# First of five convolution taps taken from VectorE to ScalarE in the first six quads of a softcap attention with a gated convolution behind it

## The chip, the cores and the metric

The kernel runs on one core of a Trainium2 chip. The metric is device time in microseconds (us) of one launch. The core has five engines, each with a queue of its own that it works off in order: TensorE (PE in the profile, with its weight loads as PEld), VectorE (DVE), ScalarE (ACT), GpSimd (POOL) and SyncE (SP), which here issues nearly all DMA transfers. Engines wait for each other only through semaphores; an instruction that waits holds up all that stands behind it on its engine.

## The reference, cut to what matters

```python
# q, k, v: (8, 12, 448, 64), cap = 30
scores = cap * np.tanh(np.matmul(q, k.transpose(0, 1, 3, 2)) / np.sqrt(64) / cap)
scores = scores - np.max(scores, axis=-1, keepdims=True)
attn = np.exp(scores)
attn = attn / (np.sum(attn, axis=-1, keepdims=True) + 1e-09)
x = np.matmul(attn, v)                    # then heads side by side: (8, 448, 768)
# gated convolution, conv_w: (5, 768), w_val and w_out: (768, 768)
xp = np.concatenate([np.zeros((B, K - 1, D)), x], axis=1)
gate_pre = 0
for k in range(K):                        # K = 5 taps
    gate_pre += conv_w[k][None, None, :] * xp[:, k:k + S, :]
gate = 1.0 / (1.0 + np.exp(-gate_pre))
val = x @ w_val
out = gate * val @ w_out
```

## The kernel before

**Tiling.** Heads are worked in pairs (48 pairs, `p`), two pairs make a quad (24 quads, `s`), and three quads make one batch element (8 batches, `b`). For a pair, q and k are loaded (`qkn`) and turned by a 32x32 block transpose on DVE (`qkt`, L515). From pair 9 on, q and k are split into a high and a low part (`qkh` by ACT at L525, `qkl` by DVE at L425, a helper's line that also makes `xl` and `g_l`). TensorE makes score tiles of 128 rows into PSUM (`pss`, L542; the remaining rows of a quad at L553), ACT takes tanh (L558, and L569 for the remaining rows) and exp (L562, L573) into `pt`, DVE adds some of them up (`pa`, L586, L589), and TensorE forms the sums of the rows (`psz`, L610) and the products with v (`psa`, `psz`, L636). DVE turns the sums (`zt`, L641), inverts them (`rc`) and spreads them (L652). L660 and L663 multiply the attention output by them into `u`, the x of one quad, with channels on partitions: 2 channel chunks of 128 by 4 + 448 columns, the first 4 being the zeros ahead of the convolution. All quads but quad 1 use the same `u`.

**The convolution and the rest.** A quad's gate (`gate`, 128 x 2 x 448) is built chunk by chunk: the step `conv(s, n)` with n from 0 to 9 is tap `i = n % 5` of chunk `t = n // 5`. Tap 0 writes `gate = u * cw` (L688), taps 1 to 4 add `u * cw` (L690, a shifted window of `u`). All ten are on DVE. Beside it ACT and DVE split `u` into `xh` (L675) and `xl`. For a batch, TensorE multiplies xh and xl with `wv` into `pss` (L706 to L708), ACT takes the sigmoid of the gate (L694), DVE multiplies the two (L718), ACT and DVE split the product into `g_h` (L721) and `g_l`, and TensorE multiplies with `wo` (L741 to L743). ACT copies the result (L750), and SP stores it. PSUM has three `pss` buffers, which scores, remainder, value and output tiles use in turn.

**The weights** arrive in 12 pieces as 64-bit floats in the first 120 us and are split on the way: SP loads `w_raw`, ACT makes two pieces of it (L311, L312), and DVE the parts that TensorE reads (L315, L316, then L319, L320, L323 with `w_late`). There is one buffer of each kind, so the next load of `w_raw` starts when L316 of the piece before has read it.

**The order.** Every step stands in a table (`PAIR`, `QUAD`, `BATCH`, `ONCE`) with a number. All steps are sorted by that number and emitted in this order, and each engine keeps it as its queue. Nothing is moved afterwards. The numbers are measured in pairs: step `conv` number n of quad s comes at `2 s` plus the table's row n. For quad 2 the table's third column holds these, in the order in which they come:

```python
# n:  0         1         5         2         6         3         7 ...
#  1.321381  1.919916  2.164879  2.18007   2.209755  2.224579  2.308679
```

Quad 2 lies at 4 plus that, so its n = 5 (tap 0 of chunk 1) at 6.165 and n = 6 (tap 1 of chunk 1) at 6.210. For quad 4 (column 5) n = 5 lies at 12.279 and n = 6 at 12.400.

Of the kernel before, what the change touches and what calls it, by code (L numbers as in the profile page):

```python
# [12 lines left out]
AF = mybir.ActivationFunctionType  # L13
# [12 lines left out]
NXX, NPT, NG = 3, 8, 3  # L26
NPRE, NLATE, NPLAIN, NTWO = 3, 4, 9, 16
NADD = (0, 0, 0, 1, 2)
BY_DMA = tuple(range(4, 12))
ON_VECTOR = (0, 1, 2, 3)  # L30

# [255 lines left out]
def shifted(late, n):  # L287

    return late.bitcast(I32)[..., 1:2 * n:2]
# [91 lines left out]
def fast_path(tc, io, u0, q, k, v, w_val, conv_w, w_out, out, capt):  # L381

    nc = tc.nc
# [15 lines left out]
    with ExitStack() as ctx:  # L399
# [37 lines left out]
        cw = cpool.tile([P, KW, NCC], F32, name="cw")  # L437
# [17 lines left out]
        def late_tile():  # L455
            return wsc.tile([P, 2, 4 * NH + 2], U16, name="w_late")

        def late_load(n):
            if n in BY_DMA:
                w, g, nh, _ = wsteps[n]  # L460
                wlate[n] = late_tile()
                nc.sync.dma_start(
                    wlate[n][:, :, 1:1 + 4 * NH], quad_rows(w.bitcast(U16), g)[:, :, nh * 2 * DM:(nh + 1) * 2 * DM]
                )

        def weight_first(n):
            _, g, nh, w = wsteps[n]
            t = wsc.tile([P, 2, NH], I32, name="w_t")
            mid = None if n in BY_DMA else late_tile().bitcast(I32)[:, :, :NH]
            c = slice(2 * g, 2 * g + 2)  # L470
# [13 lines left out]
        def weight_third(n):  # L484
            last = wstate.pop(n)[2]
            if n in BY_DMA:
                last(shifted(wlate.pop(n), NH))
# [87 lines left out]
        def adds(s):  # L575
            return NADD[s] if s < len(NADD) else NT

# [76 lines left out]
        def u_of(s):  # L654
            return u1 if s == 1 else u0
# [11 lines left out]
        def late(s):  # L667
            return s >= NLATE and s % (NXX + 1) == NLATE % (NXX + 1)
# [12 lines left out]
        def conv(s, n):  # L681
            t, i = divmod(n, KW)
            if n == 0:
                gates[s] = scratch["late"].tile([P, 2, S], F32, name="gate", bufs=1) if late(s) else wk.tile([P, 2, S], F32, name="gate", bufs=NG)
            c = s % NQ * 2 + t
            g, u = gates[s][:, t], u_of(s)[:, t, i:i + S]
            if i == 0:
                nc.vector.tensor_scalar_mul(g, u, cw[:, 0, c:c + 1])  # L688
            else:
                nc.vector.scalar_tensor_tensor(g, u, cw[:, i, c:c + 1], g, ALU.mult, ALU.add)  # L690

# [77 lines left out]
        def put(table, steps, count, unit, col):  # L769
# [9 lines left out]
        ), NP, 1, column)  # L779
        put(QUAD, dict(  # L780
            rest=rest, rest_tanh=rest_tanh, rest_exp=rest_exp, sums=sums, av=av, turn_sums=turn_sums, recip=recip, spread=spread, mul=mul, x_hi=x_hi, x_lo=x_lo, conv=conv,
        ), NP // 2, 2, quad_column)
        put(BATCH, dict(
# [186 lines left out]
```

## Time and profile before

| | |
|---|---|
| median of 3 runs | 689.72 us (689.52 to 689.75) |
| profiled execution, its own time | 689.57 us |
| its span, first to last instruction | 687.7 us |
| granted TensorE clock, mean | 0.99 |
| DVE busy in the span | 560.0 us |
| ACT busy in the span | 502.1 us |

In rows of the timeline the first number is the start and the second the length, both in us, then engine, line, operation, what is written and read, and how many instructions the row merges; a bracket at the end is the time that the engine stood idle just before, and what ended it. An instruction's length is longer than its step to the next one where the two overlap. In the chain of waits a piece is start, length, and what the end hung on in that time.

### The profile page before, as it was taken

The page shows a single profiled execution, that of the slowest core. Times are in us where ns is not written, and L with a number is a line of the kernel's source. Part 1 is how long each engine was busy: PE and PEld are TensorE (multiplying, and loading weights), DVE is VectorE, ACT ScalarE, POOL GpSimd, SP SyncE. Part 2 cuts the span into 40 slices and gives each one's busy share as a digit, 9 for nine tenths or more (in the row PEclk, how much of TensorE's full clock was granted, in tenths as well). Part 3 has the DMA queues.
Part 4 walks back from the last instruction along what each step waited for, and adds up shares of the span by engine and source line. Part 5 has one row for each costly group of instructions (what it writes and reads, how often), then busy time and mean ns, then how long its engine had stood idle before and what let it go on. Part 6 is the DMA issues. An engine that isn't in the chain of part 4 may idle for free.

```text
span 687.7 us, 11825 instructions
## 1 busy us (share of the span) xinstructions
PE 659.3 (96%) x4698; PEld 467.7 (68%) x4698; DVE 560.0 (81%) x779; ACT 502.1 (73%) x538; POOL 0.4 (0%) x7
## 2 busy tenths in 40 slices
PE   4787999999999999999999999999999999999996
PEld 1221584587597686786686696876766878767996
DVE  3899999999978889987979877988879896897530
ACT  5579769889684898777797695886788785975110
POOL 0000000000000000000000000000000000000000
PEclk9899999999999999999999999999999999999999
DMA  7769888433343432250334430423235332111001
GB/s 117 166 164 218 226 223 229 96 67 60 80 91 71 91 68 67 61 104 15 68 78 91 100 68 18 106 57 68 44 65 113 80 78 39 51 38 60 0 25 72
DMA packets 235166, 60.66 MB, mean 88 GB/s; under 512 B 226400, under 2 KB 226400, under 8 KB 235104
## 3 DMA queue, kind: packets, MB, share of 16 engines
q1 hardware_dynamic: 233248, 59.61, 39.1%
q8 instruction: 39, 0.64, 0.4%
q10 hardware_dynamic: 1856, 0.23, 0.3%
q14 instruction: 23, 0.19, 0.1%
HBM read 48.79 MB, written 11.01 MB: 87 GB/s over the span
## 4 chain that ended last, share of the span: by engine, by line
PE 75%; DVE 5%; ACT 3%; DMA 1%; issue 1%; SPq 0%; DVEq 0%; ACTq 0%
PE pss L542 10%; PE psa L636 9%; PE pss L706 8%; PE pss L741 7%; PE pss L708 7%; PE pss L707 7%; PE pss L743 7%; PE pss L742 7%; PE psz L636 7%; PE psz L610 3%; PE pss L553 2%; DVE pa L586 1%; DVE gate L690 1%; ACT pt L558 1%; ACT pt L562 1%; DVE pa L589 1%
## 5 line engine op out<-in xcount | busy, mean ns | idle before, releaser
L558 ACT ACTIVATE pt<-pss,rc 128x896 f32<-128x896 f32 x144 | 140.0, 1004 | 68.5 <-PE pss L542 44.6
L562 ACT ACTIVATE pt<-pt,capt 128x896 f32<-128x896 f32 x144 | 145.6, 1042 | 0.6
L690 DVE SCALAR_TENSOR_TENSOR gate<-u,cw,gate 128x448 f32<-128x448 f32 x192 | 125.9, 674 | 1.7
L741 PE MATMUL pss<-wo,g_h 128*128 128x384 f32 x336 | 114.9, 342 | 0.0
L743 PE MATMUL pss<-wo,g_l 128*128 128x384 f32 x336 | 113.8, 339 | 0.0
L742 PE MATMUL pss<-wo,g_h 128*128 128x384 f32 x336 | 113.6, 338 | 0.0
L706 PE MATMUL pss<-xh,wv 128*128 128x448 f32 x288 | 105.9, 368 | 0.0
L708 PE MATMUL pss<-xl,wv 128*128 128x448 f32 x288 | 104.3, 362 | 0.0
L707 PE MATMUL pss<-xh,wv 128*128 128x448 f32 x288 | 104.3, 362 | 0.0
L741 PEld LDWEIGHTS pss<-wo,g_h 128*128 128x128 f32 x336 | 63.1, 188 | 9.0 <-ACT pt L558 6.4
L636 PE MATMUL psa<-pt,vn 128*32 128x448 f32 x576 | 69.2, 547 | 0.0
L636 PE MATMUL psz<-pt,vn 128*32 128x448 f32 x576 | 64.8, 541 | 1.4 <-DVE zt L641 1.4
L750 ACT COPY osb<-pss 128x768 f32<-128x768 f32 x28 | 22.3, 798 | 57.0 <-PE pss L743 56.0
L743 PEld LDWEIGHTS pss<-wo,g_l 128*128 128x128 f32 x336 | 63.1, 188 | 0.6 <-DVE g_l L425 0.6
L742 PEld LDWEIGHTS pss<-wo,g_h 128*128 128x128 f32 x336 | 63.1, 188 | 0.4 <-DVE wo L323 0.3
L706 PEld LDWEIGHTS pss<-xh,wv 128*128 128x128 f32 x288 | 54.0, 187 | 12.9 <-ACT pt L558 5.3
L515 DVE STREAM_TRANSPOSE qkt<-qkn 128x896 f32<-128x896 f32 x47 | 51.6, 1104 | 6.7 <-DMA qkn<-in_k_dram 3.8
L708 PEld LDWEIGHTS pss<-xl,wv 128*128 128x128 f32 x288 | 54.0, 188 | 3.8
L707 PEld LDWEIGHTS pss<-xh,wv 128*128 128x128 f32 x288 | 54.0, 188 | 3.5
L718 DVE TENSOR_TENSOR gate<-pss,gate 128x896 f32<-128x896 f32 x24 | 26.1, 1088 | 31.2 <-PE pss L708 31.2
L586 DVE TENSOR_TENSOR pa<-pt 128x896 f32<-128x896 f32 x42 | 45.3, 1078 | 7.5 <-ACT pt L562 7.5
L542 PE MATMUL pss<-qkh 64*128 64x448 f32 x234 | 48.4, 406 | 0.5 <-ACT pt L558 0.5
(86 smaller groups left out, 931.9 us busy)
## 6 DMA issues: line engine op xcount, KB each, us to landing
out_dram<-osb SPq DMA_DIRECT2D x28, 384.0 KB, 2.6
qkn<-in_q_dram SPq DMA_DIRECT2D x188, 56.0 KB, 2.3
qkn<-in_k_dram SPq DMA_DIRECT2D x188, 56.0 KB, 2.3
vn<-in_v_dram SPq DMA_DIRECT2D x96, 96.0 KB, 2.5
w_raw<-in_moe_w_val_dram SPq DMA_DIRECT2D x6, 768.0 KB, 4.7
w_raw<-in_moe_w_out_dram SPq DMA_DIRECT2D x6, 768.0 KB, 5.0
w_late<-in_moe_w_out_dram SPq DMA_DIRECT2D x6, 768.0 KB, 4.9
vh<-in_v_dram SPq DMA_DIRECT2D x48, 32.0 KB, 2.3
```

The lines of the kernel that those rows point to most:

```text
L542: nc.tensor.matmul(ps[:, j, :S], st[x][r, 1, c], st[y][r, 0], start=(n == 0), stop=(n == len(parts) - 1))
L558: nc.scalar.activation(st["p", i], st.pop(("s", i)), AF.Tanh, scale=rc8)
L562: nc.scalar.activation(t, t, AF.Exp, scale=capt)
L586: nc.vector.tensor_tensor(st["a"], st["p", 0] if i == 0 else st["a"], st["p", i + 1], op=ALU.add)
L636: nc.tensor.matmul(o, w, x, start=(q["n", t] == 1), stop=(q["n", t] == NT + 1))
L690: nc.vector.scalar_tensor_tensor(g, u, cw[:, i, c:c + 1], g, ALU.mult, ALU.add)
L706: nc.tensor.matmul(o[:, t, :S], w_h, xh, start=(c == 0), stop=False)
L707: nc.tensor.matmul(o[:, t, :S], w_l, xh, start=False, stop=False)
L708: nc.tensor.matmul(o[:, t, :S], w_h, xl, start=False, stop=(c == NCC - 1))
L741: nc.tensor.matmul(o[:, nh, :NH], g_h[:, d, s], w_h, start=(d == 0), stop=False)
L742: nc.tensor.matmul(o[:, nh, :NH], g_h[:, d, s], w_l, start=False, stop=False)
L743: nc.tensor.matmul(o[:, nh, :NH], g_l[:, d, s], w_h, start=False, stop=(d == NCC - 1))
```

## The change

The first tap (n = 0 and n = 5) of quads 0 to 5 becomes an ACTIVATE of kind Copy with a scale for each partition on ScalarE. It is emitted at the place where the multiply on VectorE was. The other 18 quads keep theirs. All later lines shift by 1 up to L687 and by 4 behind the new code, so L690 of before is L694 in the changed kernel, and the new instruction is its L690.

```diff
+NTAP = 6
...
             c = s % NQ * 2 + t
             g, u = gates[s][:, t], u_of(s)[:, t, i:i + S]
             if i == 0:
-                nc.vector.tensor_scalar_mul(g, u, cw[:, 0, c:c + 1])
+                if s < NTAP:
+                    nc.scalar.activation(g, u, AF.Copy, scale=cw[:, 0, c:c + 1])
+                else:
+                    nc.vector.tensor_scalar_mul(g, u, cw[:, 0, c:c + 1])
             else:
                 nc.vector.scalar_tensor_tensor(g, u, cw[:, i, c:c + 1], g, ALU.mult, ALU.add)
```

DVE loses 12 instructions and ACT gains 12; PE and GpSimd keep their queues, and SP's differs by a wait alone. What follows shows the queues at two places; in brackets stand the engines whose semaphore an instruction waits for.

**Quad 2, chunk 1, between two weight pieces.** DVE before: L688 is n = 5, and the three L690 behind it are n = 2, 6 and 3.

```order
L323 SCALAR_TENSOR_TENSOR wo<-w_late,w_t 128x2x384 [waits DVE_49]
L690 SCALAR_TENSOR_TENSOR gate<-u_63,cw,gate 128x448
L688 TENSOR_SCALAR gate<-u_63,cw 128x448
L690 SCALAR_TENSOR_TENSOR gate<-u_63,cw,gate 128x448 [waits DVE_49] x3
L315 TENSOR_SCALAR w_t<-w_t 128x768 [waits Activation_49]
L316 TENSOR_TENSOR wo<-w_t,w_raw 128x2x384 [waits DMAHW2_49,DVE_49,Activation_49]
L690 SCALAR_TENSOR_TENSOR gate<-u_63,cw,gate 128x448
```

DVE now:

```order
L324 SCALAR_TENSOR_TENSOR wo<-w_late,w_t 128x2x384 [waits DVE_49]
L694 SCALAR_TENSOR_TENSOR gate<-u_63,cw,gate 128x448
L694 SCALAR_TENSOR_TENSOR gate<-u_63,cw,gate 128x448 [waits DVE_49]
L694 SCALAR_TENSOR_TENSOR gate<-u_63,cw,gate 128x448 [waits Activation_49]
L694 SCALAR_TENSOR_TENSOR gate<-u_63,cw,gate 128x448 [waits DVE_49]
L316 TENSOR_SCALAR w_t<-w_t 128x768
L317 TENSOR_TENSOR wo<-w_t,w_raw 128x2x384 [waits DMAHW2_49,DVE_49]
L694 SCALAR_TENSOR_TENSOR gate<-u_63,cw,gate 128x448
```

The multiply is gone, n = 6 waits for ACT, and the weight step behind it, L316 of now, needs no wait for ACT of its own any more. ACT before, in the same stretch:

```order
L562 ACTIVATE pt<-pt,capt 128x896 x3
L311 ACTIVATE w_t<-w_raw 128x768 [waits DMAHW2_49,DVE_49]
L312 ACTIVATE w_raw<-w_raw 128x768 [waits Activation_49]
L694 ACT_TABLE_LOAD
L694 ACTIVATE gate<-gate 128x896 x2
L311 ACTIVATE w_t<-w_raw 128x768 [waits DMAHW0_49,DVE_49]
L312 ACTIVATE w_raw<-w_raw 128x768 [waits Activation_49]
```

ACT now:

```order
L563 ACTIVATE pt<-pt,capt 128x896 x3
L312 ACTIVATE w_t<-w_raw 128x768 [waits DMAHW2_49,DVE_49]
L313 ACTIVATE w_raw<-w_raw 128x768 [waits Activation_49]
L698 ACT_TABLE_LOAD
L698 ACTIVATE gate<-gate 128x896 x2
L690 ACTIVATE gate<-u_63,cw 128x448
L312 ACTIVATE w_t<-w_raw 128x768 [waits DMAHW0_49,DVE_49]
```

The new tap stands behind a weight piece that waits for a DMA, a table load and two sigmoids.

**Quad 4, chunk 1.** DVE before: L688 is n = 5, the L690 behind it n = 6.

```order
L641 STREAM_TRANSPOSE zt<-psz 128x448 [waits PE_49]
L646 TENSOR_SCALAR rc<-zt,guard 128x14 [waits DVE_49]
L647 RECIPROCAL rc<-rc 128x14 [waits DVE_49]
L688 TENSOR_SCALAR gate<-u_63,cw 128x448
L690 SCALAR_TENSOR_TENSOR gate<-u_63,cw,gate 128x448 [waits DVE_49]
L425 TENSOR_TENSOR qkl<-qkt,qkh 128x896 [waits Activation_49]
```

DVE now:

```order
L642 STREAM_TRANSPOSE zt<-psz 128x448 [waits PE_49]
L647 TENSOR_SCALAR rc<-zt,guard 128x14 [waits DVE_49]
L648 RECIPROCAL rc<-rc 128x14 [waits DVE_49]
L694 SCALAR_TENSOR_TENSOR gate<-u_63,cw,gate 128x448 [waits Activation_49]
L426 TENSOR_TENSOR qkl<-qkt,qkh 128x896
```

Again n = 6 waits for ACT, and the split `qkl` comes behind it. ACT before:

```order
L562 ACT_TABLE_LOAD
L562 ACTIVATE pt<-pt,capt 128x896 [waits Activation_49]
L558 ACTIVATE pt<-pss,rc_112 128x896 [waits PE_49] x5
L562 ACTIVATE pt<-pt,capt 128x896 [waits Activation_49] x2
L569 ACTIVATE pt<-pss,rc_112 128x896 [waits PE_49]
L675 CAST xh<-u_63 128x896 [waits DVE_49]
```

ACT now:

```order
L563 ACT_TABLE_LOAD
L563 ACTIVATE pt<-pt,capt 128x896 [waits Activation_49]
L559 ACTIVATE pt<-pss,rc_112 128x896 [waits PE_49]
L690 ACTIVATE gate<-u_63,cw 128x448
L559 ACTIVATE pt<-pss,rc_112 128x896 [waits PE_49] x4
L563 ACTIVATE pt<-pt,capt 128x896 [waits Activation_49] x2
L690 ACTIVATE gate<-u_63,cw 128x448 [waits DVE_49]
L570 ACTIVATE pt<-pss,rc_112 128x896 [waits PE_49]
L676 CAST xh<-u_63 128x896
```

Tap 0 of chunk 1 of quad 4 stands behind the first of five tanh, and tap 0 of chunk 0 of quad 5 ahead of the remainder's tanh and of `xh`; that one waits for the `u` that DVE writes.

## The prediction

> **What bounds the kernel now.** I read the busy table first, then the chain of waits, then the timelines of DVE, ACT and PE around the twelve places where a first tap stands.
>
> ```profile
> PE 659.3 (96%) x4698; PEld 467.7 (68%) x4698; DVE 560.0 (81%) x779; ACT 502.1 (73%) x538; POOL 0.4 (0%) x7
> ```
>
> PE is busy for 96% of the span, so work taken from DVE counts only where PE, in the end, waits for DVE. The chain shows where that still is so:
>
> ```profile
> 103.52 0.95 ACT gate L694
> ...
> 123.68 1.09 DVE qkl L425
> ...
> 129.25 1.83 PE psz L610 x12
> ```
>
> From a sigmoid at 103.5 us to 129.2 us the end hangs on ACT and then DVE; behind that it is nearly all PE. Hence a delay on DVE or ACT ahead of 129 us is paid in full, and a later one where it makes PE wait. PE cannot win it back: it is full from there.
>
> The place that matters most is the stretch on DVE and ACT from 84 to 109 us, with the PE rows that hang on it:
>
> ```profile
> 84.54 0.42 DVE L688 TENSOR_SCALAR gate<-u,cw 128x448 f32<-128x448 f32 x1
> ...
> 90.53 0.45 DVE L688 TENSOR_SCALAR gate<-u,cw 128x448 f32<-128x448 f32 x1
> 90.89 1.87 DVE L690 SCALAR_TENSOR_TENSOR gate<-u,cw,gate 128x448 f32<-128x448 f32 x3
> 92.68 0.56 DVE L315 TENSOR_SCALAR w_t<-w_t 128x768 int32<-128x768 int32 x1
> 93.32 0.96 DVE L316 TENSOR_TENSOR wo<-w_t,w_raw 128x768 fp32r<-128x768 f32 x1
> ...
> 95.80 1.09 DVE L718 TENSOR_TENSOR gate<-pss,gate 128x896 f32<-128x896 f32 x1
> ...
> 101.93 0.96 DVE L316 TENSOR_TENSOR wo<-w_t,w_raw 128x768 fp32r<-128x768 f32 x1 [0.43 <-ACT w_raw L312]
> 102.81 0.68 DVE L690 SCALAR_TENSOR_TENSOR gate<-u,cw,gate 128x448 f32<-128x448 f32 x1
> ...
> 108.34 0.64 DVE L641 STREAM_TRANSPOSE zt<-psz 128x448 f32<-128x448 f32 x1
> ```
>
> ```profile
> 91.27 0.92 ACT L311 ACTIVATE w_t<-w_raw 128x768 f32<-128x768 f32 x1 [1.76 <-DMA w_raw<-in_moe_w_out_dram]
> 92.22 0.93 ACT L312 ACTIVATE w_raw<-w_raw 128x768 f32<-128x768 f32 x1
> 93.17 1.28 ACT L694 ACT_TABLE_LOAD   x1
> 94.46 1.80 ACT L694 ACTIVATE gate<-gate 128x896 f32<-128x896 f32 x2
> 99.98 0.93 ACT L311 ACTIVATE w_t<-w_raw 128x768 f32<-128x768 f32 x1 [3.73 <-DMA w_raw<-in_moe_w_out_dram]
> ```
>
> ```profile
> 99.41 1.02 PE L542 MATMUL pss<-qkt 64*128 64x448 f32 x4
> ...
> 109.04 0.96 PE L636 MATMUL psz<-pt,vn 128*32 128x448 f32 x8 [0.71 <-DVE zt L641]
> ```
>
> DVE works without a gap from 84 to 101 us. ACT, in the same time, waits twice for weights. That looks like room on ACT, but an engine keeps its order: the new tap (tap 0 of chunk 1 of quad 2) is behind the two sigmoids of 94.46, while DVE wants its result for the second of the three taps of 90.89.
>
> **The price of one moved tap.** On DVE it gives back 0.36 us, the step from 90.53 to 90.89. No 128x448 ACTIVATE with a scale is in the trace. Its nearest rows:
>
> ```profile
> L562 ACT ACTIVATE pt<-pt,capt 128x896 f32<-128x896 f32 x144 | 145.6, 1042 | 0.6
> ```
>
> ```profile
> 131.51 0.51 ACT L729 CAST g_h<-g_h 128x384 fp32r<-128x384 f32 x1
> ```
>
> The bounds are 0.51 us (the cast, fewer columns and no scale) and 1.04 us (exp with a per-partition scale, twice the columns). The sigmoid of 103.52 has 896 columns and 0.95 us, so 512 columns more than the cast cost 0.44 us, and 64 more 0.06. The scale operand is worth 1.04 - 0.95 = 0.09. That makes 0.51 + 0.06 + 0.09 = 0.66 us, nearest the cast. Two sigmoids take 1.80 and not 1.90, so instructions overlap by 0.10 and the step is 0.56 us. A table load is not added: the Copy of L311 at 99.98 runs behind a sigmoid with none ahead of it. In all DVE is relieved of 12 x 0.36 = 4.3 us and ACT gets 12 x 0.56 = 6.7 us. Where neither is waited for, both cost nothing.
>
> **The first two quads (40 to 72 us).** Here DVE is what PE waits for, so here is the gain:
>
> ```profile
> 60.99 0.45 DVE L688 TENSOR_SCALAR gate<-u,cw 128x448 f32<-128x448 f32 x1
> ...
> 67.38 0.96 DVE L316 TENSOR_TENSOR wv<-w_t,w_raw 128x768 fp32r<-128x768 f32 x1
> ...
> 72.17 0.65 DVE L641 STREAM_TRANSPOSE zt<-psz 128x448 f32<-128x448 f32 x1 [0.50 <-PE psz L610]
> ```
>
> ```profile
> 65.60 1.64 ACT L312 ACTIVATE w_raw<-w_raw 128x768 f32<-128x768 f32 x1
> ```
>
> ```profile
> 63.60 1.86 PE L542 MATMUL pss<-qkt 64*128 64x448 f32 x4 [2.76 <-DVE qkt L515]
> 67.05 1.02 PE L542 MATMUL pss<-qkt 64*128 64x448 f32 x4
> ```
>
> Four multiplies go before the transpose that ends PE's 2.76 us, and the DMA and ACT steps between let through about three of them: PE starts 1.1 us earlier. But ACT is full up to L312 of 65.60, two new taps stand ahead of it (1.12 us), and its own earlier start gives back some 0.5. So it ends 0.6 later, at 67.9, and L316 of 67.38 moves there. The weight steps behind it keep DVE from `zt` of 72.17, which has 0.50 us to spare, until about 72.2. PE, 1.1 early, waits there. Net: 0.0, bounds -1.1 (ACT not in the way) and +0.6.
>
> **Quad 2, chunk 1: the first stall.** DVE loses the multiply of 84.54 and is 0.3 us early when the next weight load is released, so ACT's rows from 91.27 to the sigmoids are too. The sigmoids leave ACT at 94.46 + 1.80 - 0.10 - 0.30 = 95.86; the tap ends 0.66 later, at 96.5. DVE's second tap of the three began at 90.89 + 0.62 = 91.5. So DVE stands still for some 5.6 us and is 5.0 us later than before. Queued behind it: L315 and L316 of 92.68 and 93.32, hence the next `w_raw` load, hence ACT's L311 of 99.98, hence L316 of 101.93, the last tap of quad 2 at 102.81 and the sigmoid of 103.52, the head of the chain above. If that load takes as long as before the whole 5.0 stays; if it is faster, DVE's 0.43 us at 101.93 is given back: 4.6. I take 4.8. PE feels it twice: at 99.41, whose buffer L718 of 95.80 frees, and at 109.04, where it already waits 0.71 us for `zt`. Chunk 0's tap lies ahead of `xh` and is free.
>
> **Quad 3.** Its taps come in the chain's PE part and are done microseconds before they are read: 0.
>
> **Quads 4 and 5: the second stall.**
>
> ```profile
> 155.15 0.37 DVE L688 TENSOR_SCALAR gate<-u,cw 128x448 f32<-128x448 f32 x1
> 155.56 0.69 DVE L690 SCALAR_TENSOR_TENSOR gate<-u,cw,gate 128x448 f32<-128x448 f32 x1
> ...
> 163.32 0.62 DVE L660 TENSOR_TENSOR u<-psa,zt 128x448 f32<-128x448 f32 x1
> ...
> 165.75 1.09 DVE L425 TENSOR_TENSOR xl<-u,xh 128x896 fp32r<-128x896 f32 x1 [0.59 <-ACT xh L675]
> ...
> 173.05 1.09 DVE L425 TENSOR_TENSOR qkl<-qkt,qkh 128x896 fp32r<-128x896 f32 x1 [0.31 <-ACT qkh L525]
> ...
> 178.30 1.09 DVE L589 TENSOR_TENSOR pa<-pa,pt 64x896 f32<-64x896 f32 x1
> ```
>
> ```profile
> 157.24 1.89 ACT L558 ACTIVATE pt<-pss,rc 128x896 f32<-128x896 f32 x2
> ...
> 163.88 1.01 ACT L569 ACTIVATE pt<-pss,rc 128x896 f32<-128x896 f32 x1
> ...
> 172.09 0.92 ACT L525 CAST qkh<-qkt 128x896 fp32r<-128x896 f32 x1
> ```
>
> ```profile
> 179.66 0.96 PE L610 MATMUL psz<-pa,ones 128*32 128x448 f32 x8
> ```
>
> (All in times of before; both sides are shifted by the first stall.) Quad 4's tap of chunk 1 starts behind the first tanh of 157.24, at 158.1, and ends at 158.8. DVE wants it at 155.56: 3.2 us late. So is L660, which writes quad 5's `u`, ending at 167.1 and not 163.9. Quad 5's first tap waits for this on ACT ahead of L569 of 163.88, which then starts at 167.1 + 0.56 = 167.7: ACT 3.8 late. Another new tap in the same run of ACT makes it 4.4 at `qkh` of 172.09, which DVE awaits at 173.05 (0.31 us there now). DVE is dense from there to L589 of 178.30, which then ends at 183.8, and PE's sums of 179.66 read it: 4.1 us. PE's smaller waits on the way, for `qkl` and `xl`, lie inside this. Bounds: 2.5 (PE's waits for `xl` alone, if ACT catches up) and 5.
>
> **Sum.** 689.57 (the profiled execution, 0.15 below the median) + 0.0 + 4.8 + 4.1 = 698.5, beside the median 698.6 us.
>
> **A clock that falls when PE waits.** At 63.60, behind 2.76 us of waiting and little work before it, four passes took 1.86 us, at 67.05 the same four 1.02.
>
> ```profile
> 65.00:70.00 5.00, 5.00 (x38) 1.28 (x40) 4.87 (x9) 5.00 (x6) 0.00 (x0) 0.80 0.69 119
> ```
>
> The granted clock in that slice is 0.80. The new waits are some 2 us at 99.41, some 3 us at 109.04, and shorter ones in the second stall. The two groups of passes behind 63.60 lost 0.8 us each; I take 0 here, because PE is full up to the waits, and keep +1.6 for the range. The Trainium skill ("TensorE: Matmul & The Clock Gate", Part 1: The HAM clock gate) has the clock halve after an idle window of about 3.4 us and return after as long a busy one. By that rule waits of this length may escape or not, and a whole cold window would cost an estimated 1.7 us: 700.3. The trace's drop came behind a shorter gap, so it does not bear out 3.4 us as a safe length.
>
> **The rivals.**
> - *The chain takes only the first stall* (694.4 = 689.6 + 4.8): PE's work around 160 to 180 us covers the second. For it: PE is full there. Against it: 0.31 us at 173.05 is all the cover that I find. 0.14.
> - *Both stalls and the clock drop* (700.2 = 698.6 + 1.6). 0.14.
> - *Faster*: the taps are ready when DVE wants them, and the 1.1 us that PE starts earlier at 63.60 survives, 688.6. It decides if the tap of quad 2 ends before 91.5 us; by its place it cannot start before the sigmoids end. 0.04.
> - *No change*: DVE and ACT catch up before PE waits, 689.7. It needs 4.8 us of slack between 91 and 109 us, where DVE shows 0.43. 0.03.
>
> **How the numbers follow.** My forecast, 698.6 us, has 0.65, its own range 696.3 to 700.5 (the bounds of the second stall mostly). From the first rival's 694.4 less 0.6 to the clock's 700.2 plus 1.8 for a second drop: 693.8 to 702, which leaves out the last two rivals and tails, under 2 in 10. Faster by over 0.2% (1.4 us, about what a measurement of this kernel can tell from no change) has 0.02, since the 688.6 of that rival lies within the bound and only a better gain beyond; within 0.2% has 0.05; slower 0.93.
>
> **What would show it.** DVE idle for about 5.6 us at 91 us, ended by ACT's new line, and about 3.3 us near 160; the new ACTIVATE at 0.66 us; ACT waiting for DVE's `u` ahead of quad 5's tap; `zt` at 113 us where it was 108.3; PE idle at about 110. I am wrong if the wait near 91 us is short, if `zt` of 72.17 comes a microsecond earlier, or if PE at 185 us is less than 7 us behind.

## The result, and the profile after

The changed kernel takes 700.32 us (699.4 to 702.53, 4 runs) against 689.74 us (689.52 to 690.89, 4 runs): a ratio of 1.015, 95% interval 1.0133 to 1.0166, so 10.6 us slower. The profiled execution took 699.70 us with a span of 697.5 us, 9.8 longer than before.

The busy table of the page of after:

```profile
PE 663.6 (95%) x4698; PEld 468.0 (67%) x4698; DVE 556.0 (80%) x767; ACT 508.4 (73%) x550; POOL 0.4 (0%) x7
```

DVE was relieved of 4.0 us and ACT got 6.3. Neither figure is near 9.8: the time went into waiting. The view of the new line alone (shortest, median and longest duration in ns, first and last start, and who waited for it) says where:

```profile
L690 ACT ACTIVATE gate<-u,cw x12: 651/661/689, 39.6 to 177.6; 128x448 f32<-128x448 f32 x12
...
  DVE gate L694: 9.7, 3
```

Twelve new instructions of 0.66 us made DVE stand still for 9.7 us, in three waits. The first is the tap of quad 2, chunk 1. DVE of after, 91 to 115 us:

```profile
91.33 1.40 DVE L694 SCALAR_TENSOR_TENSOR gate<-u,cw,gate 128x448 f32<-128x448 f32 x2
98.10 1.28 DVE L694 SCALAR_TENSOR_TENSOR gate<-u,cw,gate 128x448 f32<-128x448 f32 x2 [5.37 <-ACT gate L690]
...
99.89 0.96 DVE L317 TENSOR_TENSOR wo<-w_t,w_raw 128x768 fp32r<-128x768 f32 x1
...
108.12 0.96 DVE L317 TENSOR_TENSOR wo<-w_t,w_raw 128x768 fp32r<-128x768 f32 x1
```

```profile
114.53 0.64 DVE L642 STREAM_TRANSPOSE zt<-psz 128x448 f32<-128x448 f32 x1
```

ACT in the same stretch:

```profile
95.71 1.79 ACT L698 ACTIVATE gate<-gate 128x896 f32<-128x896 f32 x2
97.41 0.65 ACT L690 ACTIVATE gate<-u,cw 128x448 f32<-128x448 f32 x1
106.17 0.92 ACT L312 ACTIVATE w_t<-w_raw 128x768 f32<-128x768 f32 x1 [8.11 <-DMA w_raw<-in_moe_w_out_dram]
```

The tap runs right behind the two sigmoids, and DVE starts 0.04 us after its end at 98.06. What is queued behind on DVE carries it on: the weight split, which was at 101.93, is at 108.12 (+6.19), and `zt`, which was at 108.34, at 114.53 (+6.19). ACT, the engine that was to help, then waits 8.11 us for the weight load that DVE's lateness held back. PE, whose rows follow, now waits 2.74 us at 103.50 and is 4.09 us late there (99.41 before); the 0.70 us at 115.22 are not new (0.71 before, at 109.04). A row that stood at 129.25 starts at 135.44 (+6.19):

```profile
103.50 1.54 PE L543 MATMUL pss<-qkt 64*128 64x448 f32 x4 [2.74 <-DVE gate L722]
...
115.22 0.96 PE L637 MATMUL psz<-pt,vn 128*32 128x448 f32 x8 [0.70 <-DVE zt L642]
...
135.44 0.95 PE L611 MATMUL psz<-pa,ones 128*32 128x448 f32 x4 [0.17 <-DVE pa L587]
```

The second stall is that of quads 4 and 5. DVE of after:

```profile
165.00 0.69 DVE L694 SCALAR_TENSOR_TENSOR gate<-u,cw,gate 128x448 f32<-128x448 f32 x1 [3.57 <-ACT gate L690]
...
174.13 0.69 DVE L694 SCALAR_TENSOR_TENSOR gate<-u,cw,gate 128x448 f32<-128x448 f32 x1 [0.74 <-ACT gate L690]
175.85 1.09 DVE L426 TENSOR_TENSOR xl<-u,xh 128x896 fp32r<-128x896 f32 x1 [1.03 <-ACT xh L676]
...
183.73 1.09 DVE L426 TENSOR_TENSOR qkl<-qkt,qkh 128x896 fp32r<-128x896 f32 x1 [1.60 <-ACT qkh L526]
```

and ACT:

```profile
164.31 0.66 ACT L690 ACTIVATE gate<-u,cw 128x448 f32<-128x448 f32 x1
...
173.43 0.67 ACT L690 ACTIVATE gate<-u,cw 128x448 f32<-128x448 f32 x1 [1.30 <-DVE u L661]
```

Here the two engines hand the delay to and fro: DVE waits for ACT's tap (3.57), is late with `u`, ACT waits for `u` (1.30) with its next tap, and so ACT is late with `xh` and `qkh`, which DVE waits for (1.03, 1.60). PE waits 1.66 us for `qkl` at 166.74 on the way. Its remainder tiles (L553 of before, L554 of after) show the whole:

```profile
185.06 0.98 PE L553 MATMUL pss<-qkt 64*64 64x448 f32 x8
```

```profile
195.51 0.98 PE L554 MATMUL pss<-qkt 64*64 64x448 f32 x8
```

That is +10.45, or 4.26 on top of the 6.19. The last part of the loss is early: `zt`, at 72.17 before, is at 73.45 (+1.28).

### The profile page after: what moved, and what is told of

Same layout as the page of the kernel before. It is cut to its first block, busy times and chain, and to the rows that moved or that the text cites. A ratio compares the mean times of both kernels' runs of the same rounds, so it can differ in the third digit from the quotient of the medians.

```text
span 697.5 us, 11825 instructions
## 1 busy us (share of the span) xinstructions
PE 663.6 (95%) x4698; PEld 468.0 (67%) x4698; DVE 556.0 (80%) x767; ACT 508.4 (73%) x550; POOL 0.4 (0%) x7
## 4 chain that ended last, share of the span: by engine, by line
PE 72%; DVE 6%; ACT 1%; DMA 1%; SPq 0%; issue 0%; DVEq 0%; ACTq 0%
PE pss L543 10%; PE psa L637 8%; PE pss L710 7%; PE pss L745 7%; PE pss L712 7%; PE pss L747 7%; PE pss L711 7%; PE pss L746 7%; PE psz L637 6%; PE psz L611 3%; PE pss L554 2%; DVE gate L694 1%; DVE pa L587 1%; DVE pa L590 1%; DVE qkt L516 1%; DVE qkl L426 1%
## 5 line engine op out<-in xcount | busy, mean ns | idle before, releaser
L694 DVE SCALAR_TENSOR_TENSOR gate<-u,cw,gate 128x448 f32<-128x448 f32 x192 | 126.0, 674 | 11.3 <-ACT gate L690 9.7
L637 PE MATMUL psa<-pt,vn 128*32 128x448 f32 x576 | 70.7, 554 | 0.0
L543 PE MATMUL pss<-qkt 64*128 64x448 f32 x108 | 30.6, 680 | 22.6 <-DVE guard L435 8.3
```

Of the source, the lines that this page charges most:

```text
L543: nc.tensor.matmul(ps[:, j, :S], st[x][r, 1, c], st[y][r, 0], start=(n == 0), stop=(n == len(parts) - 1))
L637: nc.tensor.matmul(o, w, x, start=(q["n", t] == 1), stop=(q["n", t] == NT + 1))
```

## The experiments

All start from the changed kernel, and most change only which taps are on ScalarE. A pair (s, t) names quad and chunk:

```diff
-NTAP = 6
+ON_SCALAR = ((s, t), ...)
...
-                if s < NTAP:
+                if (s, t) in ON_SCALAR:
```

Each set ran beside the kernel before. Its median there was 689.65 us for the runs on quads 0 and 1 tap by tap and on quad 2 early, and 689.92 us for all others.

### Without the two taps that DVE waits longest for

```diff
+ON_SCALAR = ((0, 0), (0, 1), (1, 0), (1, 1), (2, 0), (3, 0), (3, 1), (4, 0), (5, 0), (5, 1))
```

> Ten of the twelve taps on ScalarE; tap 0 of chunk 1 of quads 2 and 4 back on VectorE. Theory (two places where VectorE waits for a tap that stands too far back in ScalarE's queue): both long waits gone, the 1.3 us that the first two quads lose by 73 us stays, 691 us (690.5 to 691.8). Rival (what costs is ScalarE's load of 12 x 0.56 us, wherever it stands): ten twelfths of the loss stay, 698.5 us.

Measured: 691.85 us, ratio 1.0023 (1.0011 to 1.0035), a hair above the theory's range. Two taps of twelve carry most of the loss; a load that grows with the number of taps is not the cause. What stayed is two things. `zt` near 72 us is still late, at 73.63, and quad 5 still costs 1.0 us (PE's remainder tiles are 2.18 late where the row of 129.25 was 1.18 late). DVE of this kernel:

```profile
165.85 0.69 DVE L694 SCALAR_TENSOR_TENSOR gate<-u,cw,gate 128x448 f32<-128x448 f32 x1 [0.74 <-ACT gate L690]
167.58 1.09 DVE L426 TENSOR_TENSOR xl<-u,xh 128x896 fp32r<-128x896 f32 x1 [1.04 <-ACT xh L676]
```

### The tap of quad 2, chunk 1, alone

```diff
+ON_SCALAR = ((2, 1),)
```

> Only tap 0 of chunk 1 of quad 2 on ScalarE. Theory: one wait of 5 us on VectorE near 91 us, all of it carried to the end, 694.6 us (694.0 to 695.2). Rival (load): one twelfth of the loss, 690.5 us. Rival (the wait is partly regained behind 129 us): 692 us.

Measured: 695.19 us, ratio 1.0078 (1.0058 to 1.0099). One instruction of 0.65 us costs some 5 us. DVE and PE of this kernel:

```profile
97.63 1.28 DVE L694 SCALAR_TENSOR_TENSOR gate<-u,cw,gate 128x448 f32<-128x448 f32 x2 [5.72 <-ACT gate L690]
```

```profile
103.03 1.78 PE L543 MATMUL pss<-qkt 64*128 64x448 f32 x4 [2.96 <-DVE gate L722]
```

PE's row of 129.25 is at 134.95 (+5.70), of which 0.59 was there at 72.76 already, and the remainder tiles at 190.69 (+5.63): next to nothing of it (0.07) is given back in between.

### The tap of quad 4, chunk 1, alone

```diff
+ON_SCALAR = ((4, 1),)
```

> Only tap 0 of chunk 1 of quad 4 on ScalarE. Theory: VectorE waits 3.3 us near 155 us and TensorE falls behind by 1.8 us for qkl and more for xl of quad 5, 692.9 us (692.0 to 694.0), less than the 4.2 us of the changed kernel, since quad 5's first tap does not stand in ScalarE's queue. Rival (TensorE's work covers it): 689.7 us.

Measured: 692.27 us, ratio 1.0047 (1.0028 to 1.0065). DVE:

```profile
159.58 0.69 DVE L694 SCALAR_TENSOR_TENSOR gate<-u,cw,gate 128x448 f32<-128x448 f32 x1 [3.57 <-ACT gate L690]
```

The wait is the same 3.57 us to the digit as with all twelve. PE goes from 0.77 late at 129 us to 3.00 late at the remainder tiles: 2.2 us, a little under the 2.5 that the prediction had as the lower bound of the second stall, and not its 4.1. The rest is looked for at quad 5, further down.

### All twelve, the two taps at an earlier place

The table's number of n = 5 is lowered for the two quads, so that the tap stands right behind tap 0 of chunk 0:

```diff
-        [-.173462, -.019449, 2.164879, 3.432542, 4.279003, ...
+        [-.173462, -.019449, 1.3215, 3.432542, 3.0235, ...
```

> All twelve taps on ScalarE as in the changed kernel, with two numbers of the table changed, so that tap 0 of chunk 1 of quads 2 and 4 stands right behind tap 0 of chunk 0 in ScalarE's queue. Theory (place, not load): 690.9 us (690.2 to 691.8), what the first two quads lose. Rival (load): 700 us as the changed kernel.

Measured: 691.48 us, ratio 1.0023 (1.0012 to 1.0035), as without the two taps. All twelve instructions are on ACT, and 9 us of the loss are gone: place, not load.

### The first two quads, tap by tap

```diff
+ON_SCALAR = ((0, 0),)                # first run
+ON_SCALAR = ((0, 1),)                # second
+ON_SCALAR = ((1, 0), (1, 1))         # third
```

> Only tap 0 of chunk 0 of quad 0 on ScalarE. It stands ahead of the w_raw load of 47.4 us, so it brings that load and the w_late load behind it forward by the same 0.35 us, closer to the k loads ahead. Theory A (w_raw is slowed by w_late following sooner): w_raw still lands 4.8 us after its issue, 689.5 us (689.0 to 690.2). Theory B (w_raw is slowed by the k loads ahead of it): it takes some 6.2 us, 690.5 us. In this one and the next the landing decides, not the time.

> Only tap 0 of chunk 1 of quad 0 on ScalarE. It stands between the two loads on VectorE, so only w_late comes forward, to 2.55 us behind w_raw where it was 2.9. Theory A: w_raw takes 6.2 us and ScalarE's L312 starts 1.4 us later against the issue of w_raw, 690.6 us (689.9 to 691.3). Theory B: 4.8 us as before, 689.7 us.

> Only the two taps of quad 1 on ScalarE, with none of quad 0, so the loads near 47 us keep their distance. Theory (ScalarE is full from 52 to 72 us): its weight step L313 ends 0.6 to 1.1 us later against the landing of w_raw, VectorE's L317 behind it waits, zt near 72 us comes up to 0.6 us later, 690.2 us (689.5 to 690.9). Rival (VectorE's relief of 0.7 us reaches TensorE): 688.9 us.

Measured: 689.92 us, ratio 0.9999 (0.999 to 1.0008); 691.39 us, 1.002 (1.001 to 1.003); 690.0 us, 1.0000 (0.9991 to 1.0009). Only the tap (0, 1) shows in the time, 0.1 us above the range of theory A. In the traces two delays can be told apart, if the start is taken at the issue of the weight load near 47 us, since everything ahead of it varies by a microsecond between executions (46.73 to 48.11). "Landing" is from there to the start of ACT's first piece of that load; "split" is from there to the end of DVE's second split, the row just ahead of `zt`. For before these are 52.11 - 47.36 and 69.91 + 1.76 - 47.36:

| kernel | first taps of quads 0 and 1 on ACT | landing | split |
|---|---|---|---|
| before, and the five runs with none of them | none | 4.72 to 4.96 | 24.24 to 24.49 |
| (0, 0) | one | 4.88 | 24.38 |
| quad 1 | two | 4.78 | 25.16 |
| (0, 1) | one | 6.07 | 25.67 |
| after, and the three runs with ten or twelve taps | all four | 6.15 to 6.52 | 26.37 to 26.83 |

The rows behind it for before and for (0, 1), from the timelines of SP (its queue) and ACT:

```profile
47.36 0.58 SPq L451 DMA_DIRECT2D w_raw<-in_moe_w_val_dram  x1
...
52.11 1.65 ACT L311 ACTIVATE w_t<-w_raw 128x768 f32<-128x768 f32 x1 [4.01 <-DMA w_raw<-in_moe_w_val_dram]
```

```profile
47.94 0.58 SPq L452 DMA_DIRECT2D w_raw<-in_moe_w_val_dram  x1
...
54.01 1.56 ACT L312 ACTIVATE w_t<-w_raw 128x768 f32<-128x768 f32 x1 [4.66 <-DMA w_raw<-in_moe_w_val_dram]
```

So (0, 1) on ACT goes with a load that lands 1.3 us later (6.07 against 4.75), and quad 1's two taps, which stand ahead of the weight pieces in a full ACT queue, cost 0.85 us by themselves. They add up: 24.31 + 1.36 + 0.85 = 26.5. Theory B falls: with (0, 0) the load came closer to the k loads and still landed after 4.88 us. Of quad 1's 0.85 only 0.25 reaches `zt` (25.06 us after the issue, 24.81 before), because `zt` had 0.50 us to spare; the run's time cannot tell that from nothing.

### Does the second load slow the first?

In the kernels with (0, 1) the next load, `w_late`, was issued 2.54 us after `w_raw` instead of 2.89 (DVE had lost an instruction ahead of the split that frees it). I took that for the cause. The test keeps the two apart, by emitting DVE's weight steps two small instructions later:

```diff
+ON_SCALAR = ((0, 1),)
-    "weight_third": [-13.787764, -3.443868, -1.06549, .453446, 1.813977, ...
+    "weight_third": [-13.787764, -3.443868, -1.06549, .6466, 1.813977, ...
```

> Tap 0 of chunk 1 of quad 0 alone on ScalarE, as in the run that lost 1.4 us, with one number changed so that two short steps on VectorE (L647, L648) come ahead of the weight step that frees w_late: w_late is issued 3.0 us or more behind w_raw again. Theory (the distance of the two loads decides): w_raw lands 4.8 us after its issue, 689.8 us (689.0 to 690.5). Rival (something else in that tap's move): 6.1 us and 691.4 us.

Measured: 690.02 us, ratio 1.0007 (0.9995 to 1.0019). The time alone would bear the theory out, and the trace does not. SP and ACT of this run:

```profile
47.70 0.58 SPq L452 DMA_DIRECT2D w_raw<-in_moe_w_val_dram  x1
50.74 0.56 SPq L463 DMA_DIRECT2D w_late<-in_moe_w_val_dram  x1
```

```profile
53.77 1.55 ACT L312 ACTIVATE w_t<-w_raw 128x768 f32<-128x768 f32 x1 [4.76 <-DMA w_raw<-in_moe_w_val_dram]
```

The loads are 3.04 us apart, and the first still lands after 6.07 us. The theory falls. What made the profiled executions differ is PE. First (0, 1) alone, then (0, 1) with the loads apart:

```profile
65.47 1.87 PE L543 MATMUL pss<-qkt 64*128 64x448 f32 x4 [2.81 <-DVE qkt L516]
...
68.92 1.87 PE L543 MATMUL pss<-qkt 64*128 64x448 f32 x4
```

```profile
65.16 1.02 PE L543 MATMUL pss<-qkt 64*128 64x448 f32 x4 [2.75 <-DVE qkt L516]
...
67.00 1.02 PE L543 MATMUL pss<-qkt 64*128 64x448 f32 x4
```

Behind the same wait the clock had fallen in the one and not in the other, and `zt` came at 75.28 and 73.03. As the intervals of the two ratios overlap, the runs do not show that the edit gained anything. So the runs do not show either how much of the loss with (0, 1) comes from the later landing and how much from the clock. Why the load lands later with (0, 1) stays open. It is not the mean bandwidth: from 51 to 52 us, with the load still under way, the DMA engines of this run were 0.65 busy. Whether one slow engine of the 16, or the q and k loads issued at 51.8 us, held it up was not tried.

### Quad 2 early, and nothing else

```diff
+ON_SCALAR = ((2, 0), (2, 1))
-        [-.173462, -.019449, 2.164879, ...
+        [-.173462, -.019449, 1.3215, ...
```

> Only the two taps of quad 2 on ScalarE, tap 0 of chunk 1 moved up right behind tap 0 of chunk 0 in the order. VectorE is full from 84 to 101 us and the end hangs on what follows there, so this is where a relief could count. Theory: VectorE is 0.7 us ahead by 93 us, but the weight loads and ScalarE's steps on them let through 0.3 us: 689.4 us (688.7 to 689.9). Rival (all of it counts): 689.0 us. Rival (the loads collide as near 47 us and take it back): 690.3 us.

Measured: 689.83 us, ratio 1.0000 (0.999 to 1.001). With the stall gone, the loss is gone, and no gain from the relief of DVE in its fullest stretch is to be seen; the interval leaves room for up to 0.7 us, so the theory's 0.3 us is neither shown nor excluded. ACT of this kernel:

```profile
99.83 0.93 ACT L312 ACTIVATE w_t<-w_raw 128x768 f32<-128x768 f32 x1 [3.52 <-DMA w_raw<-in_moe_w_out_dram]
```

DVE has two multiplies less to do there, and both engines still wait for the weight loads. PE's row of 129.25 is at 129.11, which is 56.57 us behind `zt` of 72.54 (57.08 before). That is no evidence of a gain: two kernels that have the queues of before up to there took 56.70 (the next section's first) and 58.30 (its second).

### Quad 4 and quad 5

```diff
+ON_SCALAR = ((4, 1), (5, 0))        # first run
+ON_SCALAR = ((5, 0),)               # second
```

> Tap 0 of chunk 1 of quad 4 and tap 0 of chunk 0 of quad 5 on ScalarE. Theory (the two waits feed each other: VectorE late for ScalarE's tap, ScalarE then late for VectorE's u): TensorE is 3.6 us behind at 185 us against its own time at 129 us, where the tap of quad 4 alone gave 2.2, 693.7 us (692.8 to 694.6). Rival (they only add): 2.2 + 1.0 for quad 5's taps, 692.9 us.

> Only tap 0 of chunk 0 of quad 5 on ScalarE, ahead of the remainder's tanh and of xh. Theory: ScalarE reaches it about when u is written, the tap delays xh by 0.6 us and xl with it, 0.5 us at 185 us, 690.1 us (689.5 to 690.8). Rival (free): 689.7 us.

Measured: 693.57 us, ratio 1.0057 (1.0042 to 1.0072); 690.49 us, 1.001 (1.000 to 1.002). From its row of 129.25 to the remainder tiles PE loses 3.69 us with both, 0.43 with (5, 0) alone and 2.23 with (4, 1) alone: 3.69 is more than the sum, 2.66. In the kernels with no tap of quads 4 and 5 on ACT this stretch takes 55.72 to 55.83 us, so the traces can tell this. The times cannot: the ratios' excesses, 0.47% and 0.10%, add up to the 0.57% of both. ACT and DVE with both:

```profile
167.34 0.67 ACT L690 ACTIVATE gate<-u,cw 128x448 f32<-128x448 f32 x1 [1.29 <-DVE u L661]
```

```profile
158.92 0.69 DVE L694 SCALAR_TENSOR_TENSOR gate<-u,cw,gate 128x448 f32<-128x448 f32 x1 [3.58 <-ACT gate L690]
...
168.05 0.69 DVE L694 SCALAR_TENSOR_TENSOR gate<-u,cw,gate 128x448 f32<-128x448 f32 x1 [0.74 <-ACT gate L690]
169.77 1.09 DVE L426 TENSOR_TENSOR xl<-u,xh 128x896 fp32r<-128x896 f32 x1 [1.04 <-ACT xh L676]
```

DVE's `xl` with (4, 1) alone:

```profile
169.09 1.09 DVE L426 TENSOR_TENSOR xl<-u,xh 128x896 fp32r<-128x896 f32 x1
```

With (4, 1) alone DVE is late with `u`, but its own multiply follows at once, and `xl` waits for nobody (0.59 us before), so part of the delay is taken up. With (5, 0) on ACT as well the wait is taken over to ACT and comes back: the hand-over that the prediction had built the 4.1 us on. From 3.69 to the 4.26 us of the changed kernel 0.57 are left, as from 0.43 to the 1.00 of the ten taps without (2, 1) and (4, 1). That is one more step on ACT, which the prediction had for another new tap in the same run of ACT; no run has this tap alone.

### A version without the stalls, for a gain

```diff
+ON_SCALAR = ((0, 0), (0, 1), (1, 0), (1, 1), (2, 0), (2, 1), (3, 0), (3, 1), (4, 0), (4, 1))
...
-        [-.173462, -.019449, 2.164879, 3.432542, 4.279003, ...
+        [-.173462, -.019449, 1.3215, 3.432542, 3.0235, ...
...
-    "weight_third": [-13.787764, -3.443868, -1.06549, .453446, 1.813977, ...
+    "weight_third": [-13.787764, -3.443868, -1.06549, .6466, 1.813977, ...
```

> Ten taps on ScalarE, those of quads 0 to 4, with tap 0 of chunk 1 of quads 2 and 4 moved up in ScalarE's queue and the two loads kept apart as in the run before. Theory (each loss has its own cause, and all are taken away): 689.8 us (689.0 to 690.8), as before the change and no faster, since the weight loads and ScalarE's steps on them, not VectorE, set the pace to 129 us. Rival (the load on ScalarE costs by itself): 691.5 us or more. Rival (VectorE's 3.6 us of relief shows once nothing stands in the way): 688.5 us.

Measured: 691.03 us, ratio 1.002 (1.001 to 1.003). Quad 5's loss is gone (1.14 late at 129 us, 1.15 at the remainder tiles). As this stretch holds quad 3's two taps, they cost nothing, as predicted. The 1.1 us from the first two quads stays, with a landing of 6.52. The 689.8 that I expected, with a range up to 690.8, rested on the theory of the two loads, which the run with the loads apart took away. None of the versions is faster than the kernel before.

## Why the prediction came out right, step by step

The forecast was 698.6 us, the result 700.32. In the profiled execution the sum missed by 1.2 us (698.5 against 699.70): the first two quads missed by 1.28, and the other misses nearly cancel. Term by term:

| term | predicted | measured |
|---|---|---|
| one tap on ACT | 0.66, step 0.56 | 0.66; the first at 39.63 has a step of 0.56 |
| first two quads | 0.0 | 1.28 |
| quad 2, chunk 1 | 4.8 | 6.19 - 1.28 = 4.91 |
| quad 3 | 0 | 0.01 (1.15 - 1.14, the version without the stalls) |
| quads 4 and 5 | 4.1 | 10.45 - 6.19 = 4.26 |
| behind 185 us | 0 | -0.65 |
| outside the span | 0 | +0.33 |

**The first stall** was right in mechanism and size: the idle time of DVE was put at 5.6 us and was 5.37, ended by the new line. With this tap alone it costs 5 us, and at an earlier place no loss is seen. That 4.8 and 4.91 are so close is in part luck. The sigmoids of 94.46 were to come 0.3 us early; against the 1.28 us that was lost by then they came 0.03 early (95.71). So the stall itself made DVE 5.28 us late and not 5.0 (its tap of 94.20 is at 100.76). But the load behind it took 5.26 us from issue to use (100.91 to 106.17) where it had taken 5.67 (94.31 to 99.98), and DVE's wait of 0.43 at 101.93 is gone: 0.37 came back, where the sum had counted on 0.2. Nor can one profile settle tenths here: from `zt` near 72 us to the row of 129.25 the kernels without this stall took 56.57 to 58.30 us.

PE felt it otherwise than the prediction said: some 2 us were predicted at 99.41 and some 3 at 109.04. The wait at 99.41 was 2.74 us. Behind it three slow groups took 1.64 us more than before, and a wait of 0.42 at 111.73 made up the rest, so that the wait for `zt` remained at 0.70. The sum is set by DVE and came out the same.

**The second stall** likewise: 3.3 us predicted near 160, 3.57 measured. The chain over `u`, quad 5's tap, `xh` and `qkh` is shown by the run with both taps. The rival by which the chain takes only the first stall would have needed PE's work to cover this; the 2.2 us with (4, 1) alone exclude it.

**The clock** was taken as 0, with 1.6 us kept for the range. It did fall behind the new wait. The table by stretches (the last three columns are the granted clock, the DMA engines' share and GB/s) has 1.00 for before in this slice and 0.77 for after:

```profile
105.00:110.00 5.00, 4.29 (x40) 1.03 (x36) 4.97 (x8) 4.97 (x6) 0.00 (x0) 1.00 0.86 222
```

```profile
105.00:110.00 5.00, 5.00 (x29) 2.69 (x28) 4.91 (x8) 2.15 (x3) 0.00 (x0) 0.77 0.80 208
```

The groups from 103.50 on took 1.54, 1.72 and 1.34 us instead of some 1. It cost nothing, because PE waited for DVE again behind them (0.42 us at 111.73, where it had not waited before), and DVE's rows from 99.89 to 115 us show no wait at all. So the 0 was right, but not for the reason given, that PE is full up to the waits: it was full, and the clock fell. The rival that adds 1.6 us has the number of the result by accident: the missing time is elsewhere.

**The first two quads** are the mis-sized term: 0.0, with bounds of -1.1 and +0.6, and 1.28 measured. The prediction had DVE's transpose come early enough that PE's group of 63.60 starts 1.1 us earlier. The transpose, at 62.35 before, is at 62.38 and the group at 63.64, because DVE now waits for both of ACT's pieces of the load issued at 46.85 (in before only for the second, the third row here):

```profile
54.60 0.56 DVE L316 TENSOR_SCALAR w_t<-w_t 128x768 int32<-128x768 int32 x1 [1.23 <-ACT w_t L312]
55.98 0.96 DVE L317 TENSOR_TENSOR wv<-w_t,w_raw 128x768 fp32r<-128x768 f32 x1 [0.82 <-ACT w_raw L313]
```

```profile
55.18 0.96 DVE L316 TENSOR_TENSOR wv<-w_t,w_raw 128x768 fp32r<-128x768 f32 x1 [0.54 <-ACT w_raw L312]
```

Next, the prediction had ACT's second piece of the following load end 0.6 us later and DVE's split move from 67.38 to 67.9. ACT, DVE and PE of after:

```profile
67.38 1.60 ACT L313 ACTIVATE w_raw<-w_raw 128x768 f32<-128x768 f32 x1
```

```profile
69.01 0.96 DVE L317 TENSOR_TENSOR wv<-w_t,w_raw 128x768 fp32r<-128x768 f32 x1 [0.83 <-ACT w_raw L313]
...
73.45 0.65 DVE L642 STREAM_TRANSPOSE zt<-psz 128x448 f32<-128x448 f32 x1 [0.23 <-PE psz L611]
```

```profile
67.09 1.87 PE L543 MATMUL pss<-qkt 64*128 64x448 f32 x4
```

The piece was 1.78 us late, not 0.6, and the split 1.63, not 0.5. By the table of the tap-by-tap runs, DVE's chain from the load's issue was 2.06 us longer (26.37 against 24.31). Take away `zt`'s spare 0.50 and the 0.51 by which this execution issued the load earlier, and 1.05 remain; the last 0.23 are the wait for PE, whose second group ran at the low clock (1.87 us, 1.02 before). The two taps of quad 1 ahead of ACT's pieces were counted, if at 0.6 instead of 0.85. What was left out is that the trace of before had a load in flight there whose landing could move; why it moved is open.

A part of the 1.28 is chance: of the six kernels with none of these taps on ACT before has the earliest `zt` (72.17 to 73.08, mean 72.59), and the four with all of them have it at 73.45 to 73.69, mean 73.56. That is 1.0 us, about what the times have (1.1 us in the version without the stalls). The result lies within the forecast's own range of 696.3 to 700.5, but that range was taken from the second stall, which came out to 0.2 us; it was filled by another term.

**PE cannot win it back**, the prediction said. Nearly so: 0.39 of 10.46 us went near 460 us, where DVE's transpose had waited 0.58 us for a load, by the chain of waits of before and of after:

```profile
455.28 2.53 DMA qkn<-in_k_dram
459.02 1.11 DVE qkt L515
```

```profile
465.74 2.52 DMA qkn<-in_k_dram
469.09 1.11 DVE qkt L516
```

The last copy on ACT is 10.10 us late (682.50 and 692.60) and the span 9.8 longer: the remaining 0.3 us lie behind it, at the end of the program.

## What to carry to other kernels

An instruction that is moved to an idle engine at the same place in the order does not find the engine idle: it inherits what stands ahead of it in that queue, here a weight load, a table load and two sigmoids, and hands their lateness to an engine that was full. Compare the time at which the consumer wants the result with the time at which the instruction ahead on the new queue ends; two of these twelve taps were 5.4 and 3.6 us late by that, and those two and one that reads a late result made some 9 of the 10.6 us. And before relieving a full engine, see what it would wait for next: with both taps of quad 2 early it was the same weight loads, and no gain from the relief was to be seen.

## What the runs showed of the hardware that I had not expected

The weight load near 47 us (768 KB) took 4.7 to 5.0 us from issue to use in eight kernels and 6.1 to 6.5 in the six in which one 0.43 us multiply had left DVE at the moment of its issue. I found no cause.

The clock behind one and the same wait is not the same in each execution. The kernel with (2, 1) alone has the queues of before up to 84 us. In before only the group at 63.60 was slow; here both were, and `zt` waited 1.76 us for PE instead of 0.50:

```profile
62.99 1.86 PE L543 MATMUL pss<-qkt 64*128 64x448 f32 x4 [2.76 <-DVE qkt L516]
66.43 1.87 PE L543 MATMUL pss<-qkt 64*128 64x448 f32 x4
```

```profile
72.76 0.65 DVE L642 STREAM_TRANSPOSE zt<-psz 128x448 f32<-128x448 f32 x1 [1.76 <-PE psz L611]
```

`zt` came 26.03 us after the load's issue, and 24.81 in before: 1.2 us from the clock alone, in a single profile. That is as much as some of the effects looked for here, so a difference below it between two spans proves nothing; it takes durations and waits, or many runs. The Trainium skill ("TensorE: Matmul & The Clock Gate", Part 1: The HAM clock gate) says that the gate's window runs freely, so that the place of the change varies from run to run. The two traces fit that rule, but they do not show the window itself.
